# Two Fourier mixing layers and two MLP layers on one core: the four stores of a turned tile are issued two steps later

## The chip, the cores and the metric

The kernel runs on one core of a Trainium2 chip. The metric is the device time of one execution in microseconds. Five engines work beside each other, each through its own instructions in a fixed order: TensorE (PE, the matmuls), VectorE (DVE), ScalarE (ACT), GpSimd (POOL) and SyncE (SP). SP computes nothing here: it issues nearly all transfers, one after the other, and an issue whose data or buffer is not ready holds up every issue behind it. The transfers themselves run on 16 DMA engines that all issues share.

## What is computed

`x` is 2048 x 512 in float32. Two layers, each of a Fourier mixing block (A) and an MLP block (B), are applied in turn with the same weights:

```python
def _A_ref(x, dft_seq_re, dft_seq_im, dft_hid_re, dft_hid_im):
    a = jnp.einsum("bsd,ed->bse", x, dft_hid_re)
    b = jnp.einsum("bsd,ed->bse", x, dft_hid_im)
    return jnp.einsum("ts,bse->bte", dft_seq_re, a) - jnp.einsum("ts,bse->bte", dft_seq_im, b)

def _B_ref(x, w1, w2, w3, w4):
    h = _gelu(_layernorm(x, axis=-1) @ w1)
    # the four quarters of h's columns are shifted by +1, -1, +2, -2 rows
    x1 = x + hs @ w2
    return x1 + _gelu(_layernorm(x1, axis=-1) @ w3) @ w4

x = x + _A_ref(_layernorm(x), ...)
x = x + _B_ref(_layernorm(x), ...)
x = x + _A_ref(_layernorm(x), ...)
x = x + _B_ref(_layernorm(x), ...)
```

## The kernel before

**Exact enough products.** Each float32 operand of a matmul is split into a high part (a rounded copy, made by ACT) and a low part (what the copy left out, a subtraction on DVE), and `mm3` (lines 279 to 282) makes a product out of three matmuls: high times high, high times low, low times high. The second of the three is the first to read the low part of the streamed operand.

**Block A.** The rows are handled in four chunks of 512 (`NC` = 4, index `c`). A chunk has an x phase (`x_phase`) and then a y phase (`y_phase`), and after the last chunk four products with the hidden DFT follow (`hid`). The first chunk of layer 0 goes another way (`plain_phase`). The y phase runs over eight indices k, and for each over two steps, called "by1" and "by0". A step has 12 matmuls of 512 columns into four pairs of PSUM banks; "by1" writes psc and psd, "by0" psb and psa. The order of the steps is k = 0 to 7, by1 ahead of by0, except that the by1 step of k = 7 stands ahead of the by0 step of k = 6.

**The stream of weights.** Both steps of a k use the same two 512 KB blocks of the sequence DFT, which come from HBM into four raw buffers (`raw0` to `raw3`): even k use raw0 and raw1, odd k raw2 and raw3. For each step DVE subtracts the two blocks (line 232, into one of four ring buffers, `ring0` to `ring3`), ACT copies the difference into the ring's high part (line 233), and DVE writes the low part (line 243). `stream()` hands a step's ring buffer to the matmuls and, ahead of that, lets the stages run on: the subtraction for a later step is written ahead of the low part of the step before it, so on DVE L232 of one step stands in front of L243 of the step before. `issue_dma` issues the next load (line 208) as soon as, in the program's order, the last reader of its raw buffer has been written; at run time SP waits at that issue until DVE has read the buffer. So the two loads of k + 2 are issued when the by0 subtraction of k is through.

**What else goes through SP's queue in the y phase.** At k = 1 of every chunk but the first a 512 KB tile of the residual, X1, is stored to `x1d` (`rows`, line 199). In the last chunk, `turn_in` (line 607) reads a turned tile back at k = 7. Behind the weight loads come the loads of the hidden DFT (`in_hs`).

**The turned tile.** Block B needs the normalized rows of chunk 0 with rows and columns exchanged. In the last chunk's x phase ACT writes the four normalized tiles to `tmp`; at k = 0 of that chunk's y phase DVE transposes them in blocks of 32 x 32 into `turned0` (`turn_one`, line 592, four instructions), and `turn_out` (line 602) stores them to HBM so that the blocks come to stand at their places: four stores, each from 32 partitions, 256 KB in runs of 128 floats. `turned0` lies in memory that is not used otherwise until the weights w1 are split there, after the fourth product of the hidden DFT.

**Transfers and their semaphores.** Transfers are told of by eight semaphores in rotation (DMAHW0 to DMAHW7 below), so an issue may also wait for the transfer that was issued eight places before it. `y_phase` calls its hook at every by1 step, after the step's `stream()`. The statistics of the chunk before (`stats_twice`, lines 314 to 319) are run from `run_late("y")` at k = 2, and `re0s` gets `im1s` added (`add`, line 466) at k = 4.

Of the kernel before, what the change touches and what calls it, by code (L numbers as in the profile page):

```python
# [20 lines left out]
NC = S // CH  # L21
# [21 lines left out]
def spectral_mlp_kernel(ctx: ExitStack, tc: tile.TileContext, x, ws, hs, w1, w2, w34, out):  # L43
# [153 lines left out]
    def rows(sb, d, j, n, load):  # L197
        v = d[j * P : (j + n) * P, :].rearrange("(t p) d -> p t d", p=P)
        nc.sync.dma_start(*((sb, v) if load else (v, sb)))
# [229 lines left out]
    late = {}  # L429

    def plain_phase(hook):

        for k in range(NP):
            first, last = k == 0, k == NP - 1
            a = {"11": ay[k][:, 2], "22": ay[k][:, 3], "21": mid[k % 4][:, 0], "12": mid[k % 4][:, 1]}
            s = stream()
            hook(2 * k)
            jobs = ((PB, a["21"], s[:, 1]), (PA, a["11"], s[:, 1]), (PC, a["12"], s[:, 0]), (PD, a["22"], s[:, 0]))
            if first:
                mm_first(jobs[:2])  # L440
                mm_first(jobs[2:])
            else:
                for job in jobs:
                    mm_half(*job, False, False)
            s = stream()
            hook(2 * k + 1)
            mm_half(PC, a["11"], s[:, 1], False, last)
            mm_half(PD, a["21"], s[:, 1], False, last)
            mm_half(PB, a["22"], s[:, 0], False, last)
            mm_half(PA, a["12"], s[:, 0], False, last)  # L450
# [136 lines left out]
    def blocks_of(u):  # L587
        return u.rearrange("p (d a i) -> p d a i", d=KD, a=NB)

    def turn_one(t, q, u):  # L590
        v = t.rearrange("p d (a q j) -> p d a q j", a=NB, q=TC)[:, :, :, q]
        nc.vector.transpose(v, blocks_of(u))

    def turn_out(t, to=None):

        if to is None:
            count["turn"] += 1
            to = zd[count["turn"] % 2]
        z = to.rearrange("(e i) t -> i e t", i=B)
        for b in range(NB):  # L600
            v = t[b * B : (b + 1) * B].rearrange("i d (a t) -> i (d a) t", a=NB)
            nc.sync.dma_start(z[:, :, b * P : (b + 1) * P], v)

    def turn_in(dst, col):

        z = zd[count["turn"] % 2].rearrange("(d p) t -> p d t", p=P)
        nc.sync.dma_start(dst[:, :, 1, col : col + CH], z)
# [841 lines left out]
    for layer in range(LAYERS):  # L1449
# [4 lines left out]
        for c in range(NC):  # L1454
            if layer == 0 and c == 0:
# [57 lines left out]
                def hook(i):  # L1513
                    k, odd = divmod(i, 2)
                    if not i:
                        second_low(1)
                        xp_stats(1)
                        second_low(0)
                        state["two"] += 1
                        issue_dma()  # L1520
                        state["limit"] = 4
                        prefetch()
                    state["limit"] = w_items[layer]
                    if not odd:
                        if k + 1 < NP:
                            xp_norm(k + 1, 3)
                            xp_main(k + 1)
                        if not k:
                            xp_main_lows(1)
                    else:  # L1530
                        if 0 < k < NP - 1:
                            xp_main_lows(k + 1)
                        if k + 2 < NP:
                            xp_stats(k + 2)
                        if k:
                            xp_sums(k - 1)
                            xp_highs(k - 1, False)
                            xp_lows(k - 1, False)
                    w4_split(i)
# [46 lines left out]
            def hook(k):  # L1586
                if layer and c == 0:
                    for step, f in zip((1, 1, 2), (ay_sums, ay_highs, ay_lows)):
                        if k == step:
                            f(7)  # L1590
                if k == 1 and c:
                    rows(X1, x1d, (c - 1) * TC + 2, 2, False)
                if c == NC - 1 and k == 0:
                    for q in range(TC):
                        turn_one(turned0, q, tmp[:, q])
                    turn_out(turned0)
                if c == NC - 1 and k == NP - 1:
                    turn_in(ztf[0], HALO)
# [84 lines left out]
```

## Time and profile before

| | us |
|---|---|
| median of 3 runs | 1436.4 (1435.86 to 1436.93) |
| the profiled execution, its own time | 1436.16 |
| span of its instructions on the core | 1434.0 |
| TensorE busy | 1426.2 (99%) |
| VectorE busy | 1169.5 (82%) |
| ScalarE busy | 728.0 (51%) |
| GpSimd busy | 79.7 (6%) |

The granted clock of TensorE is 1.00 throughout. The transfers move 307.57 MB, and the one queue that SP issues on takes 64.9% of the 16 DMA engines' time. Times of the profile count from the first instruction. A row of a timeline gives start, duration, engine, line, operation, output and inputs, count, and in brackets how long the engine had been idle before and what ended that. The last chunk's y phase runs from 344.08 us in layer 0; in layer 1 its rows lie some 709.6 us later (the stores start at 349.98 and at 1059.56).

### The profile page before, as it was taken

To read this page: it belongs to the slowest core of one execution; us is meant where nothing else is said; L and a number is where in the kernel's file an instruction comes from. 1 tells how busy PE (TensorE), PEld (TensorE's weight loads), DVE (VectorE), ACT (ScalarE), POOL (GpSimd) and SP (SyncE) were. 2 spreads that over 40 slices of the span, in tenths; PEclk is the share of its full clock that TensorE was granted. 3 is DMA by queue.
4 is the path that set the end of the run, shared out by engine and by line. 5 is a ranking of instruction groups with operands and counts; after the bars stand their busy time and mean duration, and the time that the engine had idled before them with its cause. 6 is when DMAs were issued, how large, how long until landed. Compare 5 with 4: busy or idle time off the path is not lost.

```text
span 1434.0 us, 17354 instructions
## 1 busy us (share of the span) xinstructions
PE 1426.2 (99%) x6285; PEld 1176.5 (82%) x6285; DVE 1169.5 (82%) x1632; ACT 728.0 (51%) x974; POOL 79.7 (6%) x111
## 2 busy tenths in 40 slices
PE   9999999999999999999999999999999999999998
PEld 8888888888788888888888888888878888888887
DVE  7986998988969788656789989889889787656676
ACT  6663455455465744434555544544545565343352
POOL 2100000000002000000000000000000010000000
PEclk9999999999999999999999999999999999999999
DMA  7866666658654857944655576575786458477764
GB/s 254 274 206 205 205 194 228 208 186 282 236 162 113 282 200 264 352 156 175 215 166 191 179 233 209 175 246 186 225 280 207 140 156 298 154 243 282 244 206 161
DMA packets 127828, 307.57 MB, mean 214 GB/s; under 512 B 9216, under 2 KB 50176, under 8 KB 124544
## 3 DMA queue, kind: packets, MB, share of 16 engines
q1 hardware_dynamic: 127744, 306.48, 64.9%
q8 instruction: 49, 0.80, 0.2%
q14 instruction: 35, 0.29, 0.1%
HBM read 252.18 MB, written 54.26 MB: 214 GB/s over the span
## 4 chain that ended last, share of the span: by engine, by line
PE 91%; DVE 4%; DMA 2%; ACT 1%; issue 1%; SPq 0%; POOL 0%; DVEq 0%; ACTq 0%; POOLq 0%
PE psd L280 9%; PE psd L282 9%; PE psd L281 9%; PE psa L280 7%; PE psa L282 7%; PE psa L281 7%; PE psc L281 7%; PE psc L282 7%; PE psc L280 7%; PE psb L281 7%; PE psb L280 7%; PE psb L282 7%; DMA raw<-in_ws 1%; DVE ring L243 1%; DMA raw<-in_hs 0%
## 5 line engine op out<-in xcount | busy, mean ns | idle before, releaser
L226 ACT CAST ring<-raw 128x1024 fp32r<-128x1024 f32 x127 | 132.9, 1052 | 78.4 <-PE psd L282 39.5
L243 DVE TENSOR_TENSOR ring<-raw,ring 128x1024 fp32r<-128x1024 f32 x126 | 153.4, 1220 | 13.5 <-ACT ring L226 13.3
L280 PE MATMUL psd<-ring,rr 128*128 128x512 f32 x208 | 80.9, 389 | 0.0
L281 PE MATMUL psd<-ring,rr 128*128 128x512 f32 x208 | 80.9, 389 | 0.0
L282 PE MATMUL psd<-ring,rr 128*128 128x512 f32 x208 | 80.9, 389 | 0.0
L233 ACT CAST ring<-ring0f 128x1024 fp32r<-128x1024 f32 x28 | 29.5, 1054 | 60.0 <-DVE ring0f L232 60.0
L320 POOL TENSOR_TENSOR rs<-ve,mhalf 128x4 f32<-128x4 f32 x16 | 25.9, 1616 | 612.9 <-DVE nm L319 612.9
L633 ACT ACTIVATE tmp<-rest 128x512 f32<-128x512 f32 x30 | 19.0, 632 | 73.0 <-DVE rest L466 72.7
L243 DVE TENSOR_TENSOR ring<-ring1f,ring 128x512 fp32r<-128x512 f32 (+1 forms) x56 | 53.3, 951 | 0.7 <-ACT ring L229 0.7
L281 PE MATMUL psb<-ring,ay 128*128 128x512 f32 x128 | 50.0, 391 | 2.3 <-DVE ring L243 2.3
L299 POOL TENSOR_TENSOR rs<-ve,mhalf 128x2 f32<-128x2 f32 (+1 forms) x33 | 28.2, 853 | 413.0 <-DVE nb L298 413.0
L328 ACT ACTIVATE tmp<-xs,nb,rs 128x512 f32<-128x512 f32 x56 | 43.3, 810 | 15.3 <-POOL nb L300 14.1
L282 PE MATMUL psb<-ring,ay 128*128 128x512 f32 x128 | 49.8, 389 | 0.0
L280 PE MATMUL psb<-ring,ay 128*128 128x512 f32 x128 | 49.8, 389 | 0.0
L280 PE MATMUL psc<-ring,ay 128*128 128x512 f32 x128 | 49.8, 389 | 0.0
L281 PE MATMUL psc<-ring,ay 128*128 128x512 f32 x128 | 49.8, 389 | 0.0
L282 PE MATMUL psc<-ring,ay 128*128 128x512 f32 x128 | 49.8, 389 | 0.0
L282 PE MATMUL psa<-ring,ay 128*128 128x512 f32 x126 | 49.0, 389 | 0.0
L281 PE MATMUL psa<-ring,ay 128*128 128x512 f32 x126 | 49.0, 389 | 0.0
L280 PE MATMUL psa<-ring,ay 128*128 128x512 f32 x126 | 49.0, 389 | 0.0
L280 PE MATMUL psd<-ring,ay 128*128 128x512 f32 x126 | 49.0, 389 | 0.0
L281 PE MATMUL psd<-ring,ay 128*128 128x512 f32 x126 | 49.0, 389 | 0.0
(666 smaller groups left out, 4429.5 us busy)
## 6 DMA issues: line engine op xcount, KB each, us to landing
raw<-in_ws SPq DMA_DIRECT2D x183, 512.0 KB, 4.9
w4r<-w4d SPq DMA_DIRECT2D x66, 512.0 KB, 4.5
raw<-in_hs SPq DMA_DIRECT2D x56, 512.0 KB, 3.7
w3b<-w3d SPq DMA_DIRECT2D x14, 1792.0 KB, 8.1
w3d<-w3b SPq DMA_DIRECT2D x5, 1792.0 KB, 6.9
x1d<-tmp SPq DMA_DIRECT2D x12, 512.0 KB, 6.4
xs<-x1d SPq DMA_DIRECT2D x12, 512.0 KB, 5.1
w4d<-w4in SPq DMA_DIRECT2D x11, 512.0 KB, 4.9
```

Of the source, the lines that this page charges most:

```text
L226: nc.scalar.copy(dest[:, a:b, 0], r[0][:, a:b])
L233: nc.scalar.copy(dest[:, :, 0], lo)
L243: nc.vector.tensor_tensor(lo, src, hi.bitcast(F32), op=ALU.subtract)
L280: nc.tensor.matmul(o, lh, rh, start=first, stop=False, skip_group_check=more)
L281: nc.tensor.matmul(o, lh, rl, start=False, stop=False, skip_group_check=more)
L282: nc.tensor.matmul(o, ll, rh, start=False, stop=last, skip_group_check=more)
L299: nc.gpsimd.tensor_tensor(rs[:, :n], ve[:, :n], mhalf[:, 0, :n], op=ALU.pow)
L320: nc.gpsimd.tensor_tensor(rs, ve, mhalf[:, :, :2], op=ALU.pow)
L328: nc.scalar.activation(o, s, AF.Identity, bias=mr[2], scale=mr[1])
L633: nc.scalar.activation(g_of, ps_of, AF.Gelu_apprx_tanh)
```

## The change

The transposes stay at k = 0. The call that stores `turned0` moves from k = 0 to k = 2, the third y step by1, behind what that step's `stream()` has issued.

```diff
@@ -1593,6 +1593,7 @@
                 if c == NC - 1 and k == 0:
                     for q in range(TC):
                         turn_one(turned0, q, tmp[:, q])
+                if c == NC - 1 and k == 2:
                     turn_out(turned0)
                 if c == NC - 1 and k == NP - 1:
                     turn_in(ztf[0], HALO)
```

On SP, in the last chunk's y phase of layer 0 (the raw buffers hold weight blocks, `x1d` is the residual's tile, `zd1` the turned tile in HBM), the difference of the two orders:

```order
+L208 DMA raw0_184<-in_ws 128x1024
+L208 DMA raw1_185<-in_ws 128x1024
+L199 DMA x1d_76<-tmp_68 128x2x512
+L208 DMA raw2_186<-in_ws 128x1024
+L208 DMA raw3_187<-in_ws 128x1024
 L602 DMA zd1_78<-turned0_157 32x16x128 x4
-L208 DMA raw0_184<-in_ws 128x1024
-L208 DMA raw1_185<-in_ws 128x1024
-L199 DMA x1d_76<-tmp_68 128x2x512
-L208 DMA raw2_186<-in_ws 128x1024
-L208 DMA raw3_187<-in_ws 128x1024
```

The two loads of k = 4 (raw0, raw1), the x1d store and the two loads of k = 5 (raw2, raw3) now stand ahead of the four stores; the loads of k = 6 follow right behind them. Layer 1 has the same difference. The waits of the changed kernel's SP at the same place, from the loads of k = 5 to the loads of k = 7:

```order
L208 DMA raw2_186<-in_ws 128x1024 [waits DMAHW7_49,DMAHW2_49,DVE_49]
L208 DMA raw3_187<-in_ws 128x1024 [waits DMAHW3_49]
L602 DMA zd1_78<-turned0_157 32x16x128 x3
L602 DMA zd1_78<-turned0_157 32x16x128 [waits DMAHW4_49]
L208 DMA raw0_184<-in_ws 128x1024 [waits DMAHW5_49,DVE_49]
L208 DMA raw1_185<-in_ws 128x1024 [waits DMAHW6_49]
L208 DMA raw2_186<-in_ws 128x1024 [waits DMAHW7_49,DVE_49]
L208 DMA raw3_187<-in_ws 128x1024 [waits DMAHW0_49]
```

Of the stores only the fourth waits, for the semaphore of the first load of k = 4; the first store waited for DVE in the kernel before. On DVE nothing moves; its order from the last row of the statistics on is, before and after:

```order
L319 TENSOR_SCALAR nm_2737<-mv_2732 128x2
L232 TENSOR_TENSOR ring0f_177<-raw1_185,raw0_184 128x2x512
L243 TENSOR_TENSOR ring3_182<-ring3f_183,ring3_182 128x2x512
L232 TENSOR_TENSOR ring1f_179<-raw1_185,raw0_184 128x2x512
L243 TENSOR_TENSOR ring0_176<-ring0f_177,ring0_176 128x2x512
L232 TENSOR_TENSOR ring2f_181<-raw3_187,raw2_186 128x2x512
L243 TENSOR_TENSOR ring1_178<-ring1f_179,ring1_178 128x2x512
L232 TENSOR_TENSOR ring3f_183<-raw3_187,raw2_186 128x2x512
L243 TENSOR_TENSOR ring2_180<-ring2f_181,ring2_180 128x2x512
L466 TENSOR_TENSOR rr00f_161<-rr00f_161,rr11f_167 128x2x512
L232 TENSOR_TENSOR ring0f_177<-raw1_185,raw0_184 128x2x512
L243 TENSOR_TENSOR ring3_182<-ring3f_183,ring3_182 128x2x512
```

The first L232 here is the by1 subtraction of k = 4, and the L243 behind it the low part of the by0 step of k = 3; the last two rows are the same for k = 6 and k = 5.

## The prediction

> **What bounds the kernel now.** I read the page of the profile first, then who waited for whom on TensorE, then the timelines of PE, DVE and SP round the two waits that this shows.
>
> ```profile
> span 1434.0 us, 17354 instructions
> PE 1426.2 (99%) x6285; PEld 1176.5 (82%) x6285; DVE 1169.5 (82%) x1632; ACT 728.0 (51%) x974; POOL 79.7 (6%) x111
> PE psb L281 <- DVE ring L243: 2.3, 2, 1.4
> ```
>
> TensorE is busy 99% of the span. The last line (of the waits: total us, times, longest us) says that in the whole kernel it waits for DVE's low parts twice, 2.3 us in all. So only what makes TensorE wait, or wait less, moves the end. Both waits lie in the y phase of the last chunk, one in each layer, which is where the change is:
>
> ```profile
> 360.42 0.39 PE L280 MATMUL psc<-ring,ay 128*128 128x512 f32 x1
> 363.14 0.39 PE L280 MATMUL psb<-ring,ay 128*128 128x512 f32 x1
> 364.39 0.50 PE L281 MATMUL psb<-ring,ay 128*128 128x512 f32 x1 [0.86 <-DVE ring L243]
> 364.73 0.39 PE L282 MATMUL psb<-ring,ay 128*128 128x512 f32 x1
> 375.40 0.39 PE L281 MATMUL psb<-ring,ay 128*128 128x512 f32 x1
> ...
> 1072.72 0.39 PE L280 MATMUL psb<-ring,ay 128*128 128x512 f32 x1
> 1074.55 0.50 PE L281 MATMUL psb<-ring,ay 128*128 128x512 f32 x1 [1.44 <-DVE ring L243]
> 1074.89 0.40 PE L282 MATMUL psb<-ring,ay 128*128 128x512 f32 x1
> ```
>
> I call the two steps of one y index a pair: pair 3 starts at 360.42 (its "by1" step), and 12 matmuls later, at 363.14, comes its "by0" step. 12 matmuls in 2.72 us make 0.227 us each. From 363.14 to 364.73 two matmuls should take 0.45 us and took 1.59: the stall of layer 0 is worth 1.14 us. In layer 1 it is 2.17 less 0.45, 1.72 us. Together 2.86 us, more than the 2.3 us of the wait line, because the first matmul after a wait is longer (0.50). That is all that can be won here: 0.2% of the time, which is also about what a measurement of this kernel can tell from no change.
>
> Why does DVE come late? Its rows in layer 0:
>
> ```profile
> 360.67 0.16 DVE L319 TENSOR_SCALAR nm<-mv 128x2 f32<-128x2 f32 x1
> 361.97 1.23 DVE L232 TENSOR_TENSOR ring0f<-raw,raw 128x1024 f32<-128x1024 f32 x1 [1.14 <-DMA raw<-in_ws]
> 363.12 1.22 DVE L243 TENSOR_TENSOR ring<-ring3f,ring 128x1024 fp32r<-128x1024 f32 x1
> 371.07 1.21 DVE L466 TENSOR_TENSOR rr00f<-rr00f,rr11f 128x1024 f32<-128x1024 f32 x1
> 372.20 1.22 DVE L232 TENSOR_TENSOR ring0f<-raw,raw 128x1024 f32<-128x1024 f32 x1
> ```
>
> The low part that pair 3's by0 step needs (L243, ring3) stands in DVE's order behind the subtraction for pair 4 (L232, ring0f). That one needs both 512 KB weight loads of pair 4, and sits 1.14 us for the second of them. So a late pair of loads holds TensorE up one step earlier than its own. Now SP and the landings (answers on DMA issues, one issue to a window: KB each, then us from issue to landing):
>
> ```profile
> 349.98 3.15 SPq L602 DMA_DIRECT2D zd<-turned  x4
> 351.87 1.26 SPq L602 DMA_DIRECT2D zd<-turned  x1
> 353.36 1.17 SPq L208 DMA_DIRECT2D raw<-in_ws  x1
> 354.57 0.89 SPq L208 DMA_DIRECT2D raw<-in_ws  x1
> 357.90 0.33 SPq L208 DMA_DIRECT2D raw<-in_ws  x1
> 365.92 0.38 SPq L208 DMA_DIRECT2D raw<-in_ws  x1
> 1064.07 1.22 SPq L208 DMA_DIRECT2D raw<-in_ws  x1
> ```
>
> ```profile
> zd<-turned SPq DMA_DIRECT2D x1, 256.0 KB, 4.7
> raw<-in_ws SPq DMA_DIRECT2D x1, 512.0 KB, 7.3
> raw<-in_ws SPq DMA_DIRECT2D x1, 512.0 KB, 4.9
> raw<-in_ws SPq DMA_DIRECT2D x1, 512.0 KB, 7.9
> ```
>
> In order these are the fourth store (351.87, down at 356.6), pair 4's second load (354.57, down at 361.85, where DVE's wait ends), pair 6's second load with nothing ahead of it (365.92, 4.9 us), and pair 4's second load of layer 1 (1064.07, down at 1072.0). Behind the stores a load takes 7.3 to 7.9 us, alone 4.9. The DVE subtraction that frees the slots of pair 4 ends just before 353.36, so the stores cost SP next to nothing in layer 0. What they take is the DMA engines.
>
> **The change, part by part.** Nothing is added or removed; eight issues (four a layer) go behind five others: pair 4's two loads, the x1d store of 512 KB and pair 5's two loads.
>
> *Pair 4's loads lose the stores ahead of them.* They go out at 353.36 as now (DVE frees the slots), into engines that have only finished pair 3. With 4.9 to 6.3 us to land (the second figure from an earlier chunk, below) both are there by 360.1, before DVE is through with its statistics at 360.8 (360.67 and 0.16). Then L232 starts at 360.8 in place of 361.97, and the low part behind it ends 2.37 us later (361.97 to 364.34 now), at 363.2. TensorE wants it at 363.37 (363.14 and one matmul). Margin 0.2 us: the stall goes, in layer 1 by the same spacing. Gain 2.86 us.
>
> *SP's own queue.* The stores' transposes end at 349.95, so at their new place they wait for nothing on DVE. The fourth waits for the DMA eight issues ahead of it, which is now a pair 4 load, down by then. Four issues took 3.15 us; from 358.7 (357.90 and two issues) they end near 362. Behind them in the queue stand pair 6's loads, which wait for DVE to free their slots at pair 4's by0 subtraction, 1.2 us earlier than today's 365.5: 364.3. So SP holds nobody up; I cost it at nothing, and its cover is 2.3 us.
>
> *The readers of the stores.* The turned z is read back at L607, at 381.98 in the profile of before. Even on the worst count below the stores are down by 371: nothing.
>
> *Pair 6's loads get the stores ahead of them.* This is what is late next. When must they be down? TensorE wanted the low part of pair 5's by0 step at 375.40, which is 374.26 without the stall. In DVE's order it stands again behind the subtraction of the pair after (372.20 now), and ends 2.37 us after that starts, so both loads of pair 6 must be down by 371.8. For what stands in the queue ahead I use chunk 2 of the same layer, which has the same loads and x1d store and no turned stores:
>
> ```profile
> 253.48 0.68 SPq L208 DMA_DIRECT2D raw<-in_ws  x1
> 254.21 0.43 SPq L199 DMA_DIRECT2D x1d<-tmp  x1
> 258.86 0.44 SPq L208 DMA_DIRECT2D raw<-in_ws  x1
> ```
>
> ```profile
> raw<-in_ws SPq DMA_DIRECT2D x1, 512.0 KB, 6.3
> x1d<-tmp SPq DMA_DIRECT2D x1, 512.0 KB, 6.9
> raw<-in_ws SPq DMA_DIRECT2D x1, 512.0 KB, 7.1
> ```
>
> So even without the turned stores, pair 5's second load takes 7.1 us behind the x1d store. Issued at 358.3 it is down at 365.4 (DVE wants it near that time, and has a further 1.3 us before TensorE would feel it). The four stores, issued right behind it, move only as the engines come free. How fast do such stores move? The rates of three stretches with nearly only such stores (last number: GB/s):
>
> ```profile
> 351.50:353.50 2.00, 2.00 (x10) 1.62 (x10) 2.00 (x3) 0.79 (x2) 0.00 (x0) 1.00 0.92 198
> 1060.50:1062.50 2.00, 2.00 (x10) 1.65 (x9) 2.00 (x3) 1.06 (x1) 0.00 (x0) 1.00 0.93 211
> 555.50:557.50 2.00, 2.00 (x11) 1.65 (x10) 2.00 (x4) 1.82 (x3) 0.00 (x0) 1.00 1.15 346
> 361.00:363.00 2.00, 2.00 (x11) 1.65 (x10) 1.03 (x1) 0.00 (x0) 1.04 (x2) 1.00 1.04 418
> ```
>
> The last is loads, for comparison. The first two are the stores of today, issued to nearly idle engines: 1.05 MB at about 205 GB/s is 5.1 us. The third is the like set of four stores of hc, issued long before the engines reached them: 346 GB/s, 3.0 us. At the new place the stores are issued from 358.7 on and the engines come free up to 365.4, so the third row is the nearest and I take 3.0 us: down at 368.4. Then pair 6. A second load came down 5.3 us after the last store today (361.85 less 356.57), and 4.9 us after the x1d store in chunk 2 (265.96 less 261.1): I take 4.9, which gives 373.3. That is 1.5 us after 371.8, and with the 0.1 us of the long first matmul a new stall of 1.6 us, one in each layer (layer 1 has the same spacing): 3.2 us.
>
> Bounds of the new stall: none, if pair 6 comes as alone (issued by 364.7, 4.9 us, down at 369.6); and 4.0 us a layer, if the stores run at 205 GB/s and the loads need 5.3 us behind them (365.4 + 5.1 + 5.3 = 375.8).
>
> [...]
>
> *Sum.* -2.86 + 3.2 = +0.3 us on the profiled execution's 1436.16 us. The median of the runs, 1436.4, is 0.24 us above that one, so I forecast 1436.7: the wait moves two pairs on and keeps about its size.
>
> **The rivals.**
> *The stall simply goes* (pair 6 is down by 371.8 in layer 0 and 709.6 us later in layer 1). For it: pair 6 is issued 5.6 us after the first store where pair 4 was issued 3.4 us after it, and alone it would have 2 us to spare. Against it: three other transfers still stand ahead of the stores, and chunk 2 shows how late the last of them is. Time 1436.4 - 2.86 = 1433.5.
> *The stall grows*, on the other side: the stores start only behind pair 5's late loads and still move at 205 GB/s. For it: two of the three rows have that rate, and each write in these rows is followed by loads that come 5 us after it. Against it: the one set that waited in the queue was quick. At its bound, 8.0 - 2.86 = 5.1 us slower, 1441.5. It decides the sign by over 0.2% once each new stall is over 2.9 us, that is once pair 6's second load is down later than 374.6.
>
> **How the numbers follow.** The forecast (a new stall between 0.6 and 2.8 us a layer, 1434.7 to 1439.1) gets 0.58, as it takes the middle row at each step. The stall that goes, with under 0.6 us left (1433.5 to 1434.7), gets 0.20; a third of that may read as faster by 0.2%, since its end lies on that limit. The stall that grows (above 1439.2) gets 0.22. That makes faster 0.07, same 0.71, slower 0.22. The range, 1433.9 to 1440.2, leaves about 0.1 out on either side.
>
> **What would show it.** In the trace after: TensorE's waits at pair 3's by0 step gone in both layers; pair 4's second load down before 360.8; the stores issued from 358.7; pair 6's loads issued near 364.3, with 7 us or more to land; a new wait of TensorE on L243 at pair 5's by0 step, ahead of which DVE waits at L232 for a load. The gain would be whole if DVE's L232 of pair 6 starts right after L466. I am wrong in the model of the queue if pair 6 lands in under 7 us, and wrong on the first step if pair 4's loads still take 7 us, which would put the delay on the x1d store.

## The result, and the profile after

| | before | after |
|---|---|---|
| median of 20 runs each, on the same chips | 1437.15 us (1435.74 to 1438.46) | 1434.61 us (1433.71 to 1436.71) |
| ratio | | 0.9984, interval 0.9977 to 0.9991 |
| the profiled execution, its own time | 1436.16 us | 1433.71 us |
| its span | 1434.0 us | 1431.6 us |

The change made the kernel faster by 0.16%, some 2.3 us by the ratio (the medians lie 2.5 us apart). The forecast was 1436.7 us, 0.3 us slower; the measured median lies inside the stated range, but on the side of the rival in which the stall simply goes (1433.5 us, or 2.86 us faster). The list of what TensorE waited for in the changed kernel:

```profile
PE psd L135 <- POOL mhalf L55: 1.4, 1, 1.4
PE psb L412 <- DVE rr L325: 0.4, 1, 0.4
```

The line that stood at 2.3 us before, psb at L281 waiting for DVE's low part, is gone from the list altogether. The first line is the wait at the kernel's start, which the kernel before has as well. TensorE's timeline at the two steps that the prediction speaks of (the by0 steps of pair 3 and of pair 5 in layer 0, then that of pair 5 in layer 1):

```profile
363.18 0.40 PE L280 MATMUL psb<-ring,ay 128*128 128x512 f32 x1
363.41 0.40 PE L281 MATMUL psb<-ring,ay 128*128 128x512 f32 x1
...
374.12 0.39 PE L280 MATMUL psb<-ring,ay 128*128 128x512 f32 x1
374.46 0.50 PE L281 MATMUL psb<-ring,ay 128*128 128x512 f32 x1
374.80 0.40 PE L282 MATMUL psb<-ring,ay 128*128 128x512 f32 x1
...
1082.89 0.39 PE L280 MATMUL psb<-ring,ay 128*128 128x512 f32 x1
1083.12 0.39 PE L281 MATMUL psb<-ring,ay 128*128 128x512 f32 x1
```

At pair 3 the second matmul follows 0.23 us behind the first: nothing is lost. At pair 5 in layer 0 (374.12) two matmuls take 0.68 us in place of 0.45, so 0.23 us of the stall has come back. The last two rows are pair 5's step in layer 1, 708.8 us on: nothing is lost there. DVE's timeline shows why:

```profile
360.75 0.16 DVE L319 TENSOR_SCALAR nm<-mv 128x2 f32<-128x2 f32 x1
360.82 1.22 DVE L232 TENSOR_TENSOR ring0f<-raw,raw 128x1024 f32<-128x1024 f32 x1
...
372.04 1.22 DVE L232 TENSOR_TENSOR ring0f<-raw,raw 128x1024 f32<-128x1024 f32 x1 [0.92 <-DMA raw<-in_ws]
```

The subtraction for pair 4 starts right behind the statistics, without a wait. The one for pair 6 now waits 0.92 us for a load, and TensorE feels 0.23 us of that. The loads and stores behind it, from SP's timeline, and under it how long each took to land, in the same order (pair 4's second load, the x1d store, pair 5's second load, the fourth store, pair 6's second load; then pair 5's second load, the fourth store and pair 6's second load in layer 1):

```profile
353.82 0.42 SPq L208 DMA_DIRECT2D raw<-in_ws  x1
354.29 0.43 SPq L199 DMA_DIRECT2D x1d<-tmp  x1
358.35 0.43 SPq L208 DMA_DIRECT2D raw<-in_ws  x1
360.47 1.41 SPq L602 DMA_DIRECT2D zd<-turned  x1
364.89 0.59 SPq L208 DMA_DIRECT2D raw<-in_ws  x1
1067.13 0.42 SPq L208 DMA_DIRECT2D raw<-in_ws  x1
1069.20 1.38 SPq L602 DMA_DIRECT2D zd<-turned  x1
1073.87 0.66 SPq L208 DMA_DIRECT2D raw<-in_ws  x1
```

```profile
raw<-in_ws SPq DMA_DIRECT2D x1, 512.0 KB, 5.9
x1d<-tmp SPq DMA_DIRECT2D x1, 512.0 KB, 6.8
raw<-in_ws SPq DMA_DIRECT2D x1, 512.0 KB, 5.7
zd<-turned SPq DMA_DIRECT2D x1, 256.0 KB, 6.7
raw<-in_ws SPq DMA_DIRECT2D x1, 512.0 KB, 7.0
raw<-in_ws SPq DMA_DIRECT2D x1, 512.0 KB, 5.7
zd<-turned SPq DMA_DIRECT2D x1, 256.0 KB, 6.7
raw<-in_ws SPq DMA_DIRECT2D x1, 512.0 KB, 6.3
```

Pair 4's second load is down at 359.7, ahead of 360.8. Pair 5's second load takes 5.7 us and not 7.1: down at 364.0 where 365.4 was forecast. The last store is down at 367.1, 3.1 us behind it, and pair 6's second load at 371.9, 4.8 us behind the store. TensorE needed it by 371.8. In layer 1 pair 5's second load takes 5.7 us too, and pair 6's is down only 4.3 us behind the last store (1080.2 against 1075.9). The rate while the stores ran (windows view, last number GB/s):

```profile
363.50:365.50 2.00, 2.00 (x10) 1.61 (x9) 2.00 (x3) 1.05 (x1) 0.00 (x0) 1.00 1.14 343
```

So the wait did move two pairs on, as forecast, but arrives there almost without size. The sum of the span: -2.86 (both old stalls) + 0.23 (the new one) + 0.2 (the L412 wait, 0.2 us before and 0.4 now, a place the change doesn't touch) = -2.4 us, which is what the span lost. This profiled execution is the fastest of the 20; the median is 0.9 us above it.

### The profile page after: what moved, and what is told of

Read it like the earlier page. It is cut to its first block, busy times and chain, and to the rows that moved or that the text cites. A ratio compares the mean times of both kernels' runs of the same rounds, so it can differ in the third digit from the quotient of the medians.

```text
span 1431.6 us, 17354 instructions
## 1 busy us (share of the span) xinstructions
PE 1425.8 (100%) x6285; PEld 1175.9 (82%) x6285; DVE 1169.2 (82%) x1632; ACT 728.6 (51%) x974; POOL 81.4 (6%) x111
## 4 chain that ended last, share of the span: by engine, by line
PE 92%; DVE 4%; ACT 1%; DMA 1%; issue 1%; POOL 0%; SPq 0%; DVEq 0%; ACTq 0%; POOLq 0%
PE psd L280 9%; PE psd L281 9%; PE psd L282 9%; PE psa L280 7%; PE psa L281 7%; PE psa L282 7%; PE psc L281 7%; PE psc L282 7%; PE psc L280 7%; PE psb L280 7%; PE psb L281 7%; PE psb L282 7%; DVE ring L243 1%; DMA raw<-in_ws 1%; DMA raw<-in_hs 0%
## 5 line engine op out<-in xcount | busy, mean ns | idle before, releaser
L243 DVE TENSOR_TENSOR ring<-raw,ring 128x1024 fp32r<-128x1024 f32 x126 | 153.4, 1219 | 13.7 <-ACT ring L226 13.6
L281 PE MATMUL psd<-ring,rr 128*128 128x512 f32 x208 | 80.9, 389 | 0.0
L243 DVE TENSOR_TENSOR ring<-ring1f,ring 128x512 fp32r<-128x512 f32 (+1 forms) x56 | 53.2, 950 | 0.7 <-ACT ring L229 0.7
L281 PE MATMUL psb<-ring,ay 128*128 128x512 f32 x128 | 50.0, 390 | 0.0
L281 PE MATMUL psc<-ring,ay 128*128 128x512 f32 x128 | 49.8, 389 | 0.0
L281 PE MATMUL psa<-ring,ay 128*128 128x512 f32 x126 | 49.1, 389 | 0.0
L281 PE MATMUL psd<-ring,ay 128*128 128x512 f32 x126 | 49.0, 389 | 0.0
```

The lines of the kernel that those rows point to most:

```text
L243: nc.vector.tensor_tensor(lo, src, hi.bitcast(F32), op=ALU.subtract)
L281: nc.tensor.matmul(o, lh, rl, start=False, stop=False, skip_group_check=more)
```

## The experiments

Two theories stood at the start. **Theory one**: the chain of the prediction holds (the stores move only behind pair 5's loads, pair 6's loads only behind the stores), and the one wrong link was the time of pair 5's second load. **Theory two**: something else made pair 6 early, so that the place of the stores hardly matters. Shifting the stores tells how much the place matters; halving and doubling them tells how much the amount does; the rest asks why pair 5 was early. All edits are against the changed kernel unless said otherwise, and all ratios against the kernel before on the same chip. A wait read from a profile is that of one execution.

### The change once more

No edit; the changed kernel again.

> The change once more, beside its neighbours on one chip. Queue theory: 0.998 of the kernel before (-2.6 us): the old stalls of 1.1 and 1.7 us gone, a new one of 0.2 us in layer 0 at pair 5's by0 step. Rival (what counts is only that the stores are queued behind other transfers and so move at 346 in place of 205 GB/s, not which loads stand behind them): the same.

Measured 1434.78 us against 1436.65, ratio 0.9986 (0.9977 to 0.9995). The effect is there again. Pair 5's second load took 5.9 and 6.1 us, again under 7.1. Pair 6's was down 3.9 and 3.8 us behind the last store, and there is no stall at pair 5's by0 step in either layer. The list of waits shows 0.3 us of DVE waits at psb and 0.3 us at psc, both in layer 1. The first lies at pair 1's by0 step, ahead of the stores; the second at pair 6's by1 step, where pair 7's loads were late. So the small rest of the stall varies in size and place from one execution to the next, and the gain stays.

### The stores another two steps later

```diff
-                if c == NC - 1 and k == 2:
+                if c == NC - 1 and k == 4:
                     turn_out(turned0)
```

> The four stores at k = 4, behind pair 7's loads, the last of the y phase; the next loads are those of the hidden DFT some 9 us later. Queue theory: no load of the y phase stands behind the stores, no stall of TensorE in the y phase at all, 0.2 us faster than the change, 2.9 us (0.2%) faster than before; the read-back at the end is not delayed. Rival: the same as the change.

Measured 1435.79 us, ratio 0.9995 (0.9986 to 1.0004): some 1 us slower than the change, and not faster. The list of waits has a new line, here, and under it stand pair 7's second load in both layers on SP's timeline with its landings, which is the load that the stores follow here:

```profile
PE psc L281 <- DVE ring L243: 1.0, 2, 0.8
```

```profile
369.05 1.39 SPq L208 DMA_DIRECT2D raw<-in_ws  x1
1079.46 0.43 SPq L208 DMA_DIRECT2D raw<-in_ws  x1
```

```profile
raw<-in_ws SPq DMA_DIRECT2D x1, 512.0 KB, 6.3
raw<-in_ws SPq DMA_DIRECT2D x1, 512.0 KB, 5.6
```

The landing of the same load in the kernel before, with nothing behind it (layer 0):

```profile
raw<-in_ws SPq DMA_DIRECT2D x1, 512.0 KB, 4.8
```

Behind these stores stand no weight loads that TensorE is short of. Yet the load *ahead* of them lands 0.7 to 1.5 us later than in the kernel before, and since pair 7's by1 step is early in the order, TensorE waits for it. The expectation missed this; it counted only what stands behind a store.

### The stores one step earlier

```diff
-                if c == NC - 1 and k == 2:
+                if c == NC - 1 and k == 1:
                     turn_out(turned0)
```

> The four stores at k = 1, behind pair 4's loads and the x1d store, ahead of pair 5's loads. Queue theory: stores down some 3.1 us after the x1d store (364.2), pair 5's second load 4.8 us behind that (369.0), 2.4 us after it is due (366.6): a stall of 2.5 us in each layer at pair 4's by0 step, 2.1 us slower than before, 4.8 us slower than the change. Rival: the stores are queued behind others here too, so the time is that of the change, -2.6 us.

Measured 1440.79 us, ratio 1.0031 (1.0020 to 1.0043): 4.4 us slower than before by the ratio, 4.1 by the medians, where some 2 us were expected. The direction is theory one's, the size is not. The waits, and then three stretches of layer 1 round the wait there (times busy; the three numbers at the end are granted clock, share of the DMA engines, GB/s):

```profile
PE psb L281 <- DVE ring L243: 4.1, 3, 2.5
```

```profile
1083.00:1084.00 1.00, 0.31 (x1) 0.31 (x2) 1.00 (x2) 0.63 (x1) 0.00 (x0) 0.64 0.02 8
1084.00:1086.00 2.00, 2.00 (x6) 1.52 (x6) 2.00 (x3) 1.05 (x1) 0.00 (x0) 0.50 0.20 31
1086.00:1088.00 2.00, 2.00 (x9) 1.66 (x8) 2.00 (x2) 0.00 (x0) 0.00 (x0) 0.83 0.88 272
```

Now pair 5's loads are late and the stall sits at pair 4's by0 step: 1.6 us in layer 0, 2.7 us in layer 1. After the second of these TensorE's granted clock is at one half for 3.41 us (1083.28 to 1086.69), 0.4 of which still lies in the wait: the other 3.0 us do half their work (a matmul every 0.43 us in place of 0.23), another 1.5 us. With 0.8 us more at the L412 wait (1.0 us there) this makes up most of the miss. That a stall is dearer than its own length stood in no term of the prediction.

### The stores one step later

```diff
-                if c == NC - 1 and k == 2:
+                if c == NC - 1 and k == 3:
                     turn_out(turned0)
```

> The four stores at k = 3, behind pair 6's loads, ahead of pair 7's, which are wanted one step sooner than the others. Queue theory: pair 6 down near 369.6, the stores 3.1 us later, pair 7's second load 4.8 us behind those (377.5), due at 374.5: a stall of 3 us in each layer at pair 6's by1 step, 3.1 us slower than before. Rival: the time of the change.

Measured 1441.41 us, ratio 1.0036 (1.0022 to 1.0050): 5.1 us slower by the ratio, 4.8 by the medians, where 3.1 were expected. The waits:

```profile
PE psc L281 <- DVE ring L243: 6.0, 2, 3.1
```

Pair 7's loads stand behind the stores here, and pair 7's by1 step stands ahead of pair 6's by0 step, so these loads are due a step sooner than pairs 5 or 6 would be: a stall of 3 us in each layer. Counted from TensorE's starts, as the prediction counts a stall, the two are worth 3.4 and 3.2 us. With two smaller waits in layer 1 that lie ahead of the stores (0.7 us at psb, 0.4 us at psa) and 0.4 us more where TensorE waits for ACT, and less the 2.86 us that went, this makes 5.2 of the 5.5 us by which the span is longer (1439.5 against 1434.0). Pair 6's second load, with the stores right behind it, took 5.8 and 6.1 us; where neither stood behind nor ahead of it, 4.8 to 5.2. At k = 2 the change stands between two bad neighbours: against the kernel before the same four stores cost 4 to 5 us a step earlier or a step later, so the place matters, and theory two falls.

### Half of the stores earlier

```diff
-    def turn_out(t, to=None):
+    def turn_out(t, to=None, blocks=range(NB)):
...
-        for b in range(NB):
+        for b in blocks:
...
                         turn_one(turned0, q, tmp[:, q])
+                    turn_out(turned0, None, (0, 1))
                 if c == NC - 1 and k == 2:
-                    turn_out(turned0)
+                    turn_out(turned0, zd[count["turn"] % 2], (2, 3))
```

> Two of the four stores at k = 0 (ahead of pair 4), two at k = 2 (ahead of pair 6). Queue theory: pair 4's second load comes 5.3 us after the second store (354.2), so at 359.5, ahead of the 360.8 at which DVE asks for it; pair 6's second load comes 1.5 us sooner than with the change, at 370.4, due 371.8. No stall of TensorE at either place, 0.998 of the kernel before, 0.2 us faster than the change. Rival (any write ahead of a load costs it the same, however small): pair 4 lands as late as before and pair 6 as late as in the change, both stalls stand: no faster than before.

Measured 1434.50 us, ratio 0.9985 (0.9975 to 0.9994): like the change. TensorE's list of waits has no line for DVE's low parts; beside the wait at the start it holds only

```profile
PE psb L280 <- ACT beside L529: 0.6, 2, 0.4
```

Pair 4's second load took 5.9 us with two stores ahead of it (7.3 with four, before, and 5.9 with none, in the change), and pair 6's second load 5.3 us (7.0 with four). So a write ahead has no fixed price, and the delay does not grow in step with the bytes either: two stores cost next to nothing, four cost 1.4 us and more. The rows suggest why: the second early store was down at 354.55, when pair 4's second load was issued at 354.37, so hardly anything of it was still ahead.

### Twice the stores

```diff
                 if c == NC - 1 and k == 2:
                     turn_out(turned0)
+                    turn_out(turned0, zd[0])
```

The second set writes the turned tile a second time, to the tensor named `zd[0]` (the first set goes to `zd[1]` in both layers); the rest of the work is the same.

> The four stores at k = 2 are issued twice, the second time to the other buffer in HBM, which nobody reads from there; the computation is unchanged. Queue theory: 1.05 MB more ahead of pair 6 at 346 GB/s is 3.0 us, pair 6's second load at 374.9 or later (SP is also busy with eight issues up to 365.3, past the 364.3 at which pair 6 could go): a stall of 3.2 to 4 us in each layer, 3.5 to 5 us slower than before (1.0025 to 1.0035). Rival: the stores are hidden where they are now; under 1 us slower than the change.

Measured 1445.68 us, ratio 1.0063 (1.0049 to 1.0077), more than expected. The waits, and a stretch of layer 0 behind the wait:

```profile
PE psb L281 <- DVE ring L243: 8.8, 3, 4.6
```

```profile
380.00:384.00 4.00, 4.00 (x11) 3.06 (x10) 4.00 (x4) 1.99 (x2) 0.00 (x0) 0.50 0.07 4
```

The stall is where the prediction put it, at pair 5's by0 step behind pair 6's loads, and is 4.8 us in layer 0 and 3.9 in layer 1. So the mechanism forecast for the change is real: the change only just has too few bytes for it. Part of the stall is SP's own time, though: with eight stores to issue it came to pair 6's first load at 367.90, where it was 364.34 in the change, and this run does not separate the two. On top come 6.83 and 3.41 us at half clock (from 377.86 and from 1094.66), of which 8.9 us lie behind the waits and lose half. Together 8.7 + 4.4 = 13.1 us against the change, and the span is 12.7 us longer (1444.3 against 1431.6).

### The x1d store ahead of pair 4's loads

Why did pair 5's second load take 5.7 us, when chunk 2 of the kernel before had 7.1? In the last chunk it has the same x1d store ahead of it. The next kernel takes that store away from there.

```diff
-                if k == 1 and c:
+                if c and k == (0 if c == NC - 1 else 1):
                     rows(X1, x1d, (c - 1) * TC + 2, 2, False)
```

> The change, and in the last chunk the x1d store goes from k = 1 to k = 0, ahead of pair 4's loads, into the 2 us in which the DMA engines had nothing to do. Queue theory: pair 5 stands behind loads alone and takes 4.9 us in place of 5.7 to 6.1, the stores start sooner by as much, pair 6's second load comes at 371.1 in place of 371.9, due 371.8: no stall, 0.2 to 0.4 us faster than the change (0.998 of before). If pair 5's time is chance and not the store ahead of it: the same as the change.

Measured 1434.51 us, ratio 0.9983 (0.9974 to 0.9992), which can't be told from the change. Pair 5's second loads (issued at 359.68 and 1068.55), with no x1d store directly ahead any more, in layers 0 and 1:

```profile
raw<-in_ws SPq DMA_DIRECT2D x1, 512.0 KB, 5.6
raw<-in_ws SPq DMA_DIRECT2D x1, 512.0 KB, 8.0
```

One took 5.6 us and the other 8.0, in one execution and with the same issues ahead. Part of the difference comes from further up the queue: pair 4's second load took 5.0 us in layer 0 and 6.1 in layer 1, so that 0.45 and 1.5 us of it were left when pair 5's second load was issued. A single landing of such a load is no constant. The expected gain over the change did not show.

### Transposes in the inner chunks

In all the runs here the second load of index 5, with the x1d store at its usual place ahead of it, took 6.5 us on average in chunks 1 and 2 (40 loads, 5.3 to 7.4), and 5.9 us in the last chunk of the seven runs with no turned stores between that store and the load (14 loads, 5.3 to 6.9). In the inner chunks SP issues it 4.5 to 5.0 us behind the x1d store, in the last one 4.1. Here the inner chunks get four transposes at k = 0 too (the results go to a temporary and are not used), to see whether DVE's work in that place makes the difference; one execution with its profile.

```diff
+                if 0 < c < NC - 1 and k == 0:
+                    for q in range(TC):
+                        turn_one(tmp[:, 0:4], q, X1[:, 0])
```

> The change, and chunks 1 and 2 get four transposes at k = 0 of their y phases as well, of other data into a tile that nobody reads at that time; so DVE issues pair 5's loads there as in the last chunk, 4.1 us after the x1d store in place of 4.95. Theory one (a load that joins the queue while the transfer ahead still runs starts without a gap): pair 5's second load in these four places comes about 10.1 us after the issue of the x1d store, as in the last chunk of the change (9.7), against 10.6 to 12.4 without them. Theory two (the last chunk's addresses make the difference): it comes at 10.6 to 12.4 as before, so takes 6.5 to 8.3 us from its own issue. The time is that of the change within 0.1%.

The time was 1436.14 us, 0.1% above the median of the change. The four loads took 6.4, 5.4, 5.7 and 6.9 us. From the issue of the x1d store these loads are down after 10.5, 9.4, 9.8 and 10.95 us, 10.2 on average, against 11.35 in the inner chunks without transposes and 10.0 in the last chunk. One of the four lies in the range that theory two named (10.6 to 12.4), the mean is that of theory one. So the time at which DVE's work lets SP issue the loads is the likelier difference, and the place in memory the less likely one. It is argued from four loads, of a kind of which the 40 spread from 9.9 to 12.4, and no run shows how the spacing of the issues makes the load shorter.

### The kernel before, with its x1d store late

This edit is against the kernel before: its turned stores stay at k = 0, and the last chunk's x1d store goes from k = 1 to k = 4.

```diff
-                if k == 1 and c:
+                if (k == 1 and 0 < c < NC - 1) or (k == 4 and c == NC - 1):
                     rows(X1, x1d, (c - 1) * TC + 2, 2, False)
```

> The kernel before (stores at k = 0), with the last chunk's x1d store moved from k = 1, right behind pair 4's loads, to k = 4, behind pair 7's. Theory one (a load is late for what stands ahead of it in the queue, so the old stalls are the stores' alone): pair 4's second load takes 7.3 to 7.9 us as before, both stalls stay, and the time is that of before within 0.5 us, or more if pair 7 is disturbed. Theory two (the x1d store right behind pair 4 costs it about 1 us, as pair 4 takes 5.8 to 6.3 us in all chunks where it stands there, and 5.0 where it doesn't): the load takes 6.3 to 6.9 us, the stalls shrink to 0.2 and 0.7 us, some 1.9 us faster than before.

Measured 1437.78 us against 1436.46, ratio 1.0008 (0.9999 to 1.0017). The waits, two of them at pair 3's by0 step in layers 0 and 1, and the landings of the second loads of pairs 4 and 7 in layer 0 (issued at 354.44 and 370.02):

```profile
PE psb L281 <- DVE ring L243: 1.5, 3, 0.6
PE psc L281 <- DVE ring L243: 1.4, 2, 0.8
```

```profile
363.95 0.50 PE L281 MATMUL psb<-ring,ay 128*128 128x512 f32 x1 [0.56 <-DVE ring L243]
1075.94 0.50 PE L281 MATMUL psb<-ring,ay 128*128 128x512 f32 x1 [0.56 <-DVE ring L243]
```

```profile
raw<-in_ws SPq DMA_DIRECT2D x1, 512.0 KB, 7.0
raw<-in_ws SPq DMA_DIRECT2D x1, 512.0 KB, 6.0
```

Pair 4's second load took 7.0 us (6.9 in layer 1) without the x1d store behind it, and 7.3 (7.9) with it. That is the upper edge of what theory two said. Counted as in the prediction, the two stalls at pair 3's by0 step are 0.83 us each, where the kernel before has 1.14 and 1.72 (the third wait at psb lies at pair 1's by0 step, ahead of the stores). So in this execution 1.7 of the 2.86 us stay with the turned stores ahead, and 1.2 us went with the x1d store behind: the stores have the larger share and not all of it. One execution of each kernel can't tell how much of the 1.2 us is chance. At its new place the x1d store made pair 7's second load 6.0 us long in both layers, in place of 4.8, and TensorE waits for that. It is the same as with the stores at k = 4, by another store.

## Why the prediction was wrong, point by point

**The old stall goes: right.** Pair 4's second load came down at 359.7, DVE began L232 at 360.82 (forecast 360.8), and the 2.86 us of both layers are gone.

**SP holds nobody up: right for the change.** The stores were issued from 358.83 to 361.88 (forecast 358.7 to 362), pair 6's second load at 364.89. It is not free in general: with the stores at k = 1, SP's issue of pair 5's first load took 2.88 us, and with eight stores the fifth took 2.98.

**The stores run at 346 GB/s behind other transfers: right.** The window shows 343, and the last store was down 3.1 us after pair 5's load (forecast 3.0). The stores issued to nearly idle engines took 5.1 us by the prediction's estimate from their 198 and 211 GB/s.

**Pair 6 lands 4.9 us after the last store: right in layer 0 of the profile, too long otherwise.** It was 4.8 us there, 4.3 in layer 1, and 3.9 and 3.8 in the second profiled execution (The change once more). Over all runs the second load behind turned stores was down 2.5 to 5.8 us after the last of them, so this distance is no constant either. The prediction named a sign of a wrong model of the queue, pair 6 landing in under 7 us: it took 7.0 us in layer 0, and 6.3 in layer 1 and in both layers of the second execution. The order in the queue held, as the shifted and doubled stores show; this distance was taken too long.

**Pair 5's second load takes 7.1 us: this is the step that failed.** It took 5.7 us in both layers, so the stores, and behind them pair 6, came 1.4 us earlier than forecast. In place of 373.3, pair 6 was down at 371.9, against 371.8 that TensorE needed; the forecast new stall of 1.6 us a layer was 0.23 us in layer 0 and nothing in layer 1. With 5.7 in place of 7.1 the prediction's own chain gives 371.9 and a stall of 0.2 us, so the mechanism was right and a term was mis-sized. In layer 1, and in the second execution (5.9 and 6.1 us), the shorter distance from the last store to pair 6 took off a further 0.6 to 1.1 us.

The prediction took one row, of another chunk, for it. More rows of that kind would not have helped. These are the landings of the same load in the kernel before, in chunks 1 and 2 of layer 0 and then of layer 1; the second is the row that the prediction used:

```profile
raw<-in_ws SPq DMA_DIRECT2D x1, 512.0 KB, 6.6
raw<-in_ws SPq DMA_DIRECT2D x1, 512.0 KB, 7.1
raw<-in_ws SPq DMA_DIRECT2D x1, 512.0 KB, 6.9
raw<-in_ws SPq DMA_DIRECT2D x1, 512.0 KB, 7.4
```

Their mean is 7.0, so all four would have given the same forecast. The 1.4 us have two sources. About 0.6 us is the place: all 40 such loads in the inner chunks average 6.5 us, and those of the last chunk, where SP issues them 4.1 us behind the x1d store and not 4.5 to 5.0, average 5.9. The prediction took the inner chunk for the last one because the same loads and the same store stand in its queue, and left the spacing out. The rest is chance: the four rows lie above the average (the same four of the changed kernel took 6.1, 6.0, 7.3 and 5.8 us), and the two of the last chunk lie below theirs. With the averages measured since (5.9 for the load, 3.1 for the stores, 4.2 for the four distances to pair 6 in the two executions of the change) the chain gives 371.5, ahead of the 371.8 at which pair 6 is due: no stall.

**The rivals.** "The stall simply goes" is what was measured, though not for its reason: pair 6's second load did queue behind the stores, for 7.0 and 6.3 us, and was 0.2 us late in layer 0 and half a microsecond early in layer 1. "The stall grows" named the right danger: with twice the stores it comes at the place forecast, with 4.8 and 3.9 us.

**The weights.** The chain adds the times of three things in a queue and compares the end with a due time 1.5 us away. Two of them, taken from rows of other places, moved by up to 1.4 and 1.1 us and decided between the forecast and the rival; the chance of 0.20 for the rival was too small for that. Pair 7's loads, which are due a step sooner, stood in no term; in the second execution TensorE waited 0.3 us for them.

## What to carry to other kernels

Here a transfer's landing time was a draw, not a constant (5.3 to 7.4 us for the same load, 40 times), and it belonged to its place (6.5 us on average in the inner chunks, 5.9 in the last): rows of the same load from another chunk, with another spacing of the issues ahead, can be off together. When the spread of such rows is as large as the margin, split the chance between "late" and "just in time". A bulk store in a queue of tight loads cost on both sides (a load took 7.0 and 6.3 us behind the four stores and 4.9 alone, another 6.3 and 5.6 us ahead of them and 4.8 alone), so it belongs where neither the loads right behind it nor the one right ahead of it are next on the critical path; here one place in five was good. And a stall of the matrix engine can cost more than its length when the clock falls: with the wait of 2.5 us it fell to 0.50 for 3.41 us, which cost another 1.5 us.

## What the runs showed of the hardware that was not expected

**A store behind a load makes the load late.** Pair 7's second load took 4.8 us in the kernel before, 6.3 and 5.6 with the four stores issued right behind it, 6.0 and 6.0 with the x1d store behind it; pair 6's 4.8 to 5.2 alone, 5.8 and 6.1 with stores behind it. A load ahead that is still on its way can do the same, so the two must be kept apart. Where pair 6's second load had 0.3 to 0.7 us to go when pair 7's was issued, pair 7's took 4.8 to 5.0 us alone and 5.6 to 6.3 with a store behind it. Where pair 6's had 2.1 to 2.7 us to go, pair 7's took 4.6 to 5.9 us with no store behind it. No run here shows by what mechanism a store delays the load ahead.

**The clock halves with a wait, but not with every wait.** A wait of 2.5 us came with 3.41 us at a granted clock of 0.50 (stores at k = 1, layer 1), those of 4.6 and 3.7 us (twice the stores) with 6.83 and 3.41 us. Waits of 3.1 and 2.9 us with the stores at k = 3 left it at 1.00; the first:

```profile
376.00:380.00 4.00, 1.29 (x6) 0.75 (x4) 2.00 (x2) 0.69 (x1) 0.00 (x0) 1.00 0.08 31
380.00:382.00 2.00, 1.58 (x7) 1.31 (x8) 2.00 (x3) 0.78 (x2) 0.00 (x0) 1.00 0.00 0
```

The traces record the fall before the wait ends: at 1083.28 us with the stores at k = 1, 2.06 us into the wait of 2.5 us, and with twice the stores at 377.86 and 1094.66 us, 3.4 and 3.6 us into those of 4.6 and 3.7 us. With twice the stores the four changes (back at full clock at 384.69 and 1098.07) lie 6.83, 709.97 and 3.41 us apart, which is 2, 208 and 1 times 3.413 us. In the kernel before the clock falls to 0.50 once, at 1432.8 us, 2.4 us after the last matmul; in the changed kernel it is still 1.00 at the end of the span, 3.6 us after the last matmul.

So the length of the wait alone does not decide: 2.5 us was once enough, and 3.1 and 2.9 us were not. What else does, no run here shows.
